# Moving the load of one batch's values behind the sort of the batch before it

## The chip, the cores and the metric

The kernel runs on one core of a Trainium2 chip. The metric is the device time of one execution in microseconds (us), median of the runs shown. The engines are named as in the profile: PE is TensorE, DVE VectorE, ACT ScalarE, POOL GpSimd, SP SyncE.

## The reference

Two stages follow each other: block-sorted attention, then a mixture of experts that every token passes through. Cut to what matters:

```python
# attention: B, H, S, D = 4, 8, 768, 64; 8 blocks of 96 tokens
P = sort_net
for _ in range(5):                       # Sinkhorn, over an 8x8 matrix per batch and head
    P = np.exp(P - P.max(-1, keepdims=True))
    P = P / (P.sum(-1, keepdims=True) + 1e-9)
    P = P / (P.sum(-2, keepdims=True) + 1e-9)
k_sorted = einsum('bhij,bhjcd->bhicd', P, k_blocks)
v_sorted = einsum('bhij,bhjcd->bhicd', P, v_blocks)
attn = softmax(q_blocks @ k_sorted^T / sqrt(D))      # inside each block
x = (attn @ v_sorted) -> (B*S, H*D) = (3072, 512)
# experts: E = 8, F = 1024
G = exp(logits - max), logits = x @ w_gate; 8 rounds of row and column scaling
out = sum_e G[:, e] * (relu(x @ w1[e]) @ w2[e])
```

All inputs and the output are float32 in HBM; the kernel works in bfloat16 with float32 accumulation.

## The kernel before

The attention stage goes batch by batch, numbered 0 to 3 in the code. Into its steps PE's work for expert 0 (`hidden0` L402, `output0` L411) on batches already attended is woven, so that PE has something to do while ACT and DVE empty its banks. Batch 0 has a prologue of its own. For batches 1 to 3 `attention` (L374) takes a plan of steps: `q` turns queries, `k` sorts keys, `s` makes scores, `m` mixes the sorted values, `t` or `T` turns the result (by PE, or by a transposing DMA from SP).

The steps around the change:

- `load_batch(bb, parts)` (L70) asks for queries, keys or values of a batch, 128 x 8 x 384 elements cast to bfloat16 on the way, by a DMA issued from POOL. Its tile `kvq` has five buffers, shared by all loads. The issue is pinned: it keeps its place in program order.
- `spread_r(bb)` (L151, by `build_r` L134) builds R, the matrices with which PE sorts keys and values of a batch: two multiplications on POOL of `Pb` (the finished P, spread over the partitions in the first stage) by a mask. They are pinned too. R has two buffers, one for even and one for odd batches.
- `sort_values(bb, bank)` (L162) sorts the values: eight matmuls on PE (L165, reading R and the loaded values), each emptied by ACT into `vs` (L167); then `hop(bb)` (L155) copies `vs` into `vsb`, eight small DMAs, four issued from SP and, for batches 2 and 3, four from POOL.
- `queries(bb, hp, bank)` (L174) reorders a pair of heads of batches 2 and 3 from the loaded queries into `qr` by a copy on POOL (L186) and turns them on PE (L190). The copies on POOL are not pinned: the scheduler puts them where it finds room between the pinned ones. `qr` has two buffers.

PE's order is pinned by hand throughout; POOL works off one queue in order, whose first member that waits holds up all behind it. At the place of the change the code runs the first steps of batch 1 (`run_both(at1, ...)`), asks for all of batch 2's loads (values, keys, queries), then for batch 3's values, spreads P for batch 2, goes on with batch 1's mixing steps, sorts the values of batch 2 and finishes batch 1 (L591 to L599). Keys and queries of batch 3 are asked for in the loop over batches 2 and 3, ahead of `spread_r(3)` (L608, L609).

Of the kernel before, what the change touches and what calls it, by code (L numbers as in the profile page):

```python
# [25 lines left out]
def kernel(  # L26
# [43 lines left out]
    def load_batch(bb, parts):  # L70
        for x, l0, n in parts:
            d, src = {"v": (vt, v), "k": (kt, k), "q": (qt, q)}[x]
            if bb not in d:
                d[bb] = kvp.tile([128, 8, 384], BF16, name="kvq", bufs=5)
            pin(nc.gpsimd.dma_start(
                out=d[bb][:, l0:l0 + n, :],
                in_=src[bb, l0:l0 + n].rearrange("h (p kk) d -> p h (kk d)", kk=6)))
# [4 lines left out]
    def load_w1(e, f0=0, f1=F):  # L82
        if e not in w1t:
            w1t[e] = wp.tile([128, 4, F], BF16, name="w1e")
        pin(nc.gpsimd.dma_start(
            out=w1t[e][:, :, f0:f1],
            in_=moe_w1[e].rearrange("(kk k) f -> k kk f", k=128)[:, :, f0:f1]))
# [63 lines left out]
    def spread_r(bb):  # L151
        for _ in build_r(bb, nc.gpsimd, 4):
            pass

    def hop(bb, pieces=None):  # L155
        for eng, i, h0, n in pieces or [(nc.gpsimd if i % 2 and bb > 1 else nc.sync, i, 0, 8)
                                        for i in range(NB)]:
            (pin if bb == 0 else lambda ins: ins)(eng.dma_start(
                out=mkap(vsbt[bb % 2], [[VW, 96], [1, 65 * n]], off=i * 520 + 65 * h0),
                in_=vs[16 * i:16 * i + 16, :, h0:h0 + n].rearrange("p kk h d -> p kk (h d)")))  # L160

    def sort_values(bb, bank):  # L162
        for h in range(8):
            vps = bank([128, 384], F32)
            pin(nc.tensor.matmul(vps, Rt[bb][:, h].rearrange("p i c -> p (i c)"),  # L165
                                 vt[bb][:, h, :], start=True, stop=True))
            nc.scalar.copy(vs[:, :, h, 0:64], vps.rearrange("p (kk d) -> p kk d", d=64))  # L167
            if h % 2:
                yield
        hop(bb)  # L170
# [203 lines left out]
    def attention(bb, bank, plan):  # L374

        def step(what, hp):
            if what == "q":
                queries(bb, hp, bank)
            elif what == "k":
                keys(bb, hp, bank)  # L380
            elif what == "s":
                scores(bb, hp, bank)
            elif what == "t":
                turn(bb, hp, bank, nc.vector.tensor_copy)
            elif what == "T":
                turn_by_dma(bb, hp)
            elif what == "x":
                next(x0)
            elif what == "L":
                logits(bb - 1, bank, range(4))  # L390
            elif what == "l":
                logits(bb, bank, (0, 1, 2) if hp == 0 else (3,))
            else:
                for h in range(2):
                    mix(bb, hp, h, bank)

        for some in plan.split():
            for x in some.split(","):
                step(x[0], int(x[1]))
            yield  # L400

    def hidden0(c0, hTs, hbank, fbs=range(8)):  # L402
        for fb in fbs:
            hps = hbank()
            for kk in range(4):
                pin(nc.tensor.matmul(hps[:, 0:384], w1t[0][:, kk, fb * 128:(fb + 1) * 128],  # L406
                                     xtT[:, kk, c0:c0 + 384], start=(kk == 0), stop=(kk == 3)))
            nc.scalar.activation(out=hTs[:, fb, 0:384], in_=hps[:, 0:384], func=AF.Relu)
            yield

    def output0(c0, hTs, obank, done, tts=range(3)):  # L411
        for tt in tts:
            oacc = obank()
            for fb in range(8):
                pin(nc.tensor.matmul(oacc, hTs[:, fb, tt * 128:(tt + 1) * 128],  # L415
                                     w2t[0][:, fb, :], start=(fb == 0), stop=(fb == 7)))
                if fb == 3:
                    yield
            done(c0 // 128 + tt, oacc)
            yield  # L420
# [10 lines left out]
    def sum_w(e):  # L431
        wct[e] = (wcq if e % 2 == 0 else wcp).tile([128, 3, 2, F // 2], BF16, name="wc")
        for kk in range(2):
            a11, a21 = (w1t[e][:, kk, f:f + 512] for f in (0, 512))
            a12, a22 = (w1t[e][:, 2 + kk, f:f + 512] for f in (0, 512))
            s1, s2, s4 = (wct[e][:, j, kk, :] for j in range(3))
            for a, b, o, c in ((a21, a22, ALU.add, s1), (s1, a11, ALU.subtract, s2),
                               (a11, a21, ALU.subtract, a21), (a12, s2, ALU.subtract, s4)):
                pin(nc.gpsimd.tensor_tensor(out=c, in0=a, in1=b, op=o))
                yield  # L440
# [105 lines left out]
    def weave(a, b, na, nb):  # L546

        t = 0
        for i in range(na):
            next(a, 0)  # L550
            while t * na < (i + 1) * nb:
                next(b, 0)
                t += 1

    with ExitStack() as c2:
        pa = c2.enter_context(tc.tile_pool(name="pa", bufs=8, space=bass.MemoryType.PSUM,
                                           reuse_waits="tile"))
        bank1 = lambda shape, dt: pa.tile(shape, dt, name="bank", tag="bank")
        ebank = lambda: bank1([128, 512], F32)
        def by_turns(x, y):  # L560
            for a, b in ((x, y), (x, y)):
                yield next(a)
                yield next(b)

        def first_two():
            yield from hidden0(384, halves[1], ebank, range(2, 8))
            for c0, hTs in ((0, halves[0]), (384, halves[1])):
                o = [output0(c0, hTs, ebank, keep, (tt,)) for tt in range(3)]
                if c0 == 0:
                    yield from by_turns(o[0], o[1])  # L570
                    yield from o[2]
                else:
                    for one in o:
                        yield from one
            for c0 in (S, S + 384):
                hTs = mps.tile([128, 8, 384], BF16, name="hTs")
                yield from hidden0(c0, hTs, ebank)
                yield from output0(c0, hTs, ebank, keep)

        ex = first_two()  # L580

        def run(n):
            for _ in range(n):
                next(ex)

        def run_both(a, counts):
            for n in counts:
                next(a, 0)
                run(n)

        at1 = attention(1, bank1, "k0 k1 q0 q1 s0 k2 q2 k3 q3 s1 s2 s3 "  # L591
                                  "m0 m1,t0 m2,t1 m3,t2 t3,l0 l3")
        run_both(at1, (1, 1, 1, 0, 1, 0, 0, 1, 0, 1, 0, 2))
        load_batch(2, [(x, 0, 8) for x in "vkq"])
        load_batch(3, [("v", 0, 8)])
        spread_r(2)
        run_both(at1, (2, 1, 1, 1))
        run_both(sort_values(2, bank1), (1, 0, 1, 0, 1))
        run_both(at1, (1, 1))  # L599
        for bb, plan, ns in (  # L600
                (2, "q0,q1,k0 k1,s0 q2,k2,s1 m0,T0 k3,s2,x0 q3,m1,T1,x0 s3,x0 m2,T2 m3,T3",
                 (6, 3, 2, 3)),
                (3, "q0,q1,k0 k1,s0 q2,k2,s1 m0,T0 k3,s2 q3,m1,T1 s3,L0 m2,T2 m3,T3",
                 (6, 4, 0, 4))):
            at1 = attention(bb, bank1, plan)
            weave(at1, ex, 5, ns[0])
            if bb + 1 < B:
                load_batch(bb + 1, [(x, 0, 8) for x in "kq"])  # L608
                spread_r(bb + 1)  # L609
            else:  # L610
                load_w1(1)
                sums = sum_w(1)
            weave(at1, ex, 3, ns[1])
            if bb + 1 < B:
                weave(sort_values(bb + 1, bank1), ex, 5, ns[2])
            else:
                for _ in sums:
                    pass
            weave(at1, ex, 1, ns[3])
        for _ in ex:  # L620
            pass
# [16 lines left out]
    def bank():  # L638
        return bk.tile([128, 512], F32, name="bk")
# [312 lines left out]
```

## Time and profile before

| | |
|---|---|
| median of 3 runs | 673.08 us (673.03 to 673.88) |
| the profiled execution, its time | 673.76 us |
| its span in the trace | 671.8 us |
| mean granted PE clock | 0.994 |
| busy: PE, DVE, POOL, ACT | 98%, 83%, 70%, 45% of the span |
| the attention stage | about the first 110 us |

In a timeline row stand the start in us from the span's start, the duration in us, engine, line, operation, the tiles written and read, the count (x), and in brackets the idle time of the engine ahead of it and what ended that. A row of waits has the engine and line that waited, what it waited for, the sum in us, how often and the longest. A row of a stretch (A:B) has its length, then busy time and count of PE, weight load, DVE, ACT and POOL, then granted PE clock, mean busy share of the DMA engines, and GB/s. A row of DMA issues has the count, KB of each, and the median us from issue to landing. In the clock row of the page each digit stands for a fortieth of the span, 9 for full speed.

### The profile page before, as it was taken

Reading aid. Unit: us, or ns where it says so; the run is one execution under the profiler, and the core shown is the slowest. Engines: PE = TensorE matmul, PEld = TensorE weight load, DVE = VectorE, ACT = ScalarE, POOL = GpSimd, SP = SyncE. Lnnn points to the kernel's source line nnn. Section 1 sums busy time; section 2 is a strip of 40 time slices with the busy share of each in tenths; the row PEclk is TensorE's granted clock in tenths of the full one; section 3 lists DMA queues with packets and bytes.
Section 4 is the critical chain, followed back from the end, with each engine's and each line's share of the span. In section 5 each row is a group of like instructions: output and inputs, shape, how many; then the busy total and the mean of one; then the engine's idle time right before and its main releaser. Section 6 shows DMA issues by size and latency. Waiting matters only on the chain.

```text
span 671.8 us, 13104 instructions
## 1 busy us (share of the span) xinstructions
PE 656.9 (98%) x5076; PEld 433.1 (64%) x5076; DVE 554.5 (83%) x1119; ACT 300.7 (45%) x535; POOL 470.5 (70%) x500
## 2 busy tenths in 40 slices
PE   7996999999999999999999999999999999999997
PEld 3763666554666666666666666666666666666666
DVE  6654566776888889898988989898989898989896
ACT  5772874477455434334333334333433343344330
POOL 4702435008997898898997898689886999646653
PEclk9997999999999999999999999999999999999999
DMA  9999996200340340031302140034003030001224
GB/s 187 175 220 133 144 138 88 48 1 2 62 64 1 63 63 1 1 64 9 55 1 35 30 63 2 1 63 63 1 0 64 6 59 1 1 1 52 76 95 157
DMA packets 39775, 38.53 MB, mean 57 GB/s; under 512 B 8512, under 2 KB 32800, under 8 KB 39712
## 3 DMA queue, kind: packets, MB, share of 16 engines
q0 software_dynamic: 26784, 27.03, 25.9%
q1 hardware_dynamic: 12816, 10.56, 6.4%
q8 instruction: 39, 0.64, 0.4%
q14 instruction: 24, 0.20, 0.1%
q10 hardware_dynamic: 112, 0.10, 0.1%
HBM read 52.45 MB, written 6.29 MB: 87 GB/s over the span
## 4 chain that ended last, share of the span: by engine, by line
PE 89%; ACT 0%; POOL 0%; DVE 0%; issue 0%; ACTq 0%
PE bk L701 38%; PE oacc L788 37%; PE oacc L415 3%; PE bk L406 3%; PE bank L415 2%; PE bank L406 2%; PE bank L244 1%; PE bk L788 1%; PE bank L226 1%; PE bank L165 1%; PE bank L204 1%; PE bk L824 1%; PE bank L190 0%; PE bank L275 0%; ACT atp L234 0%; POOL R L139 0%
## 5 line engine op out<-in xcount | busy, mean ns | idle before, releaser
L753 DVE SCALAR_TENSOR_TENSOR osbl<-oacc,glog,osbl 128x256 f32<-128x256 f32 (+1 forms) x490 | 255.9, 524 | 27.9 <-PE oacc L788 18.4
L701 PE MATMUL bk<-xtT,w1e 128*128 128x512 bf16 x504 | 148.6, 379 | 0.0
L771 POOL TENSOR_TENSOR hs<-hT 128x512 bf16<-128x512 bf16 (+2 forms) x105 | 98.4, 949 | 70.0 <-DVE hT L719 70.0
L788 PEld LDWEIGHTS <-hT 128*128 128x128 bf16 x996 | 97.4, 98 | 62.6 <-issue 0.2
L719 DVE CUSTOM_DVE_ANT_0 hT<-bk,p 128x512 bf16<-128x512 f32 x168 | 116.0, 691 | 26.1 <-PE bk L701 23.8
L788 PEld LDWEIGHTS <-hs 128*128 128x128 bf16 x996 | 97.4, 98 | 61.2 <-issue 1.6
L788 PE MATMUL oacc<-w2e,hT 128*128 128x256 bf16 x796 | 119.8, 273 | 0.0
L724 ACT COPY p<-bk 128x512 f32<-128x512 f32 x84 | 49.1, 585 | 147.5 <-PE bk L701 147.0
L771 POOL TENSOR_TENSOR hs<-hT,hs 128x512 bf16<-128x512 bf16 (+2 forms) x105 | 98.9, 950 | 4.7
L771 POOL TENSOR_TENSOR hs<-hs,hT 128x512 bf16<-128x512 bf16 (+2 forms) x105 | 99.0, 952 | 4.5 <-ACT hT L746 0.2
L701 PE MATMUL bk<-xc,wc 128*128 128x512 bf16 x336 | 99.8, 379 | 0.1
L746 ACT ACTIVATE hT<-bk 128x512 bf16<-128x512 f32 x84 | 50.1, 597 | 96.1 <-PE bk L701 96.1
L788 PE MATMUL oacc<-w2e,hs 128*128 128x256 bf16 x612 | 91.8, 273 | 0.0
L701 PEld LDWEIGHTS <-w1e 128*128 128x128 bf16 x672 | 65.7, 98 | 12.1
L719 DVE CUSTOM_DVE_ANT_0 hT<-bk,u 128x512 bf16<-128x512 f32 x84 | 58.0, 691 | 2.6 <-PE bk L701 2.6
L728 ACT COPY u<-bk 128x512 f32<-128x512 f32 x84 | 49.1, 585 | 23.9 <-PE bk L701 23.2
L733 ACT COPY p<-bk 128x512 f32<-128x512 f32 x84 | 49.2, 586 | 23.5 <-PE bk L701 23.5
L747 DVE SCALAR_TENSOR_TENSOR h<-bk,hT 128x512 bf16<-128x512 f32 x84 | 57.2, 681 | 2.6 <-ACT hT L746 2.6
L701 PEld LDWEIGHTS <-wc 128*128 128x128 bf16 x504 | 49.3, 98 | 8.1 <-issue 0.3
L788 PE MATMUL oacc<-w2s,hs 128*128 128x256 bf16 x364 | 53.3, 272 | 0.0
L701 PE MATMUL bk<-xc,w1e 128*128 128x512 bf16 x168 | 50.0, 379 | 0.0
L701 PE MATMUL bk<-xtT,wc 128*128 128x512 bf16 x168 | 50.0, 379 | 0.0
(148 smaller groups left out, 781.1 us busy)
## 6 DMA issues: line engine op xcount, KB each, us to landing
w1e<-in_moe_w_dram POOLq DMA_DIRECT2D x7, 1024.0 KB, 8.2
w2e<-in_moe_w_dram POOLq DMA_DIRECT2D x7, 1024.0 KB, 9.2
out_dram<-osbl SPq DMA_DIRECT2D x23, 256.0 KB, 2.1
kvq<-in_v_dram POOLq DMA_DIRECT2D x3, 768.0 KB, 10.1
kvq<-in_k_dram POOLq DMA_DIRECT2D x3, 768.0 KB, 11.0
vsb<-vs SPq DMA_DIRECT2D x18, 97.5 KB, 5.1
kvq<-in_q_dram POOLq DMA_DIRECT2D x4, 384.0 KB, 9.9
kvq<-in_q_dram POOLq DMA_DIRECT2D x2, 768.0 KB, 19.6
```

Of the source, the lines that this page charges most:

```text
L406: pin(nc.tensor.matmul(hps[:, 0:384], w1t[0][:, kk, fb * 128:(fb + 1) * 128], xtT[:, kk, c0:c0 + 384], start=(kk == 0), stop=(kk == 3)))
L415: pin(nc.tensor.matmul(oacc, hTs[:, fb, tt * 128:(tt + 1) * 128], w2t[0][:, fb, :], start=(fb == 0), stop=(fb == 7)))
L701: hold(nc.tensor.matmul(ps, wa[:, kk, :], xa[:, kk, :], start=(first and kk == 0), stop=(kk == 1), skip_group_check=True))
L719: nc.vector._custom_dve(TENSOR_ADD_SAT, out=out, in0=ps, in1=other, s0=TOP, s1=0.0)
L724: still(nc.scalar.copy(p1, u))
L728: still(nc.scalar.copy(u2, u))
L733: still(nc.scalar.copy(p5, v))
L746: still(nc.scalar.activation(out=c21, in_=u, func=AF.Relu))
L747: nc.vector.scalar_tensor_tensor(out=h3[e, p][:, i, :], in0=u, scalar=0.0, in1=c22, op0=ALU.max, op1=ALU.subtract)
L753: nc.vector.scalar_tensor_tensor(out=o, in0=ps, scalar=glog[:, t, e:e + 1], in1=o, op0=ALU.mult, op1=ALU.add)
L771: hold(nc.gpsimd.tensor_tensor(out=c, in0=a, in1=b, op=o))
L788: nc.tensor.matmul(ps, h[:, fb, :], w[:, fb, :], start=(first and fb == 0), stop=(fb == 3), skip_group_check=True)
```

## The change

The call that asks for batch 3's values moves from ahead of `spread_r(2)` to behind `sort_values(2, bank1)`, whose last step is the hop of batch 2. No instruction is added or taken away.

```diff
@@ -592,10 +592,10 @@
                                   "m0 m1,t0 m2,t1 m3,t2 t3,l0 l3")
         run_both(at1, (1, 1, 1, 0, 1, 0, 0, 1, 0, 1, 0, 2))
         load_batch(2, [(x, 0, 8) for x in "vkq"])
-        load_batch(3, [("v", 0, 8)])
         spread_r(2)
         run_both(at1, (2, 1, 1, 1))
         run_both(sort_values(2, bank1), (1, 0, 1, 0, 1))
+        load_batch(3, [("v", 0, 8)])
         run_both(at1, (1, 1))
         for bb, plan, ns in (
                 (2, "q0,q1,k0 k1,s0 q2,k2,s1 m0,T0 k3,s2,x0 q3,m1,T1,x0 s3,x0 m2,T2 m3,T3",
```

## The prediction

> Batches are numbered as in the code, from 0: "v3" is the load of the values of batch 3 (the fourth), R2 the spread of P for batch 2, a "hop" the copies of sorted values from vs to vsb.
>
> **What bounds the kernel now.** I read the page first, then TensorE's waits, then the queue of the engine it waits for.
>
> ```profile
> PE 656.9 (98%) x5076; PEld 433.1 (64%) x5076; DVE 554.5 (83%) x1119; ACT 300.7 (45%) x535; POOL 470.5 (70%) x500
> PEclk9997999999999999999999999999999999999999
> ```
>
> TensorE is busy 98% of the span, so nothing but a hole in its work, or a slow clock, can be won. The clock row has one digit under 9, the fourth slice (50.4 to 67.2 us). The waits of TensorE, longest first, name one hole:
>
> ```profile
> PE bank L165 <- POOL R L139: 6.2, 1, 6.2
> PE pair L298 <- DMA kvq<-in_q_dram: 1.2, 1, 1.2
> ```
>
> One wait of 6.2 us, and the next is five times smaller. L165 is the first matmul that sorts the values of batch 2, and it waits for R2, two multiplications on POOL. POOL's timeline shows why R2 is late:
>
> ```profile
> 34.13 0.88 POOL L75 DMA_DIRECT2D kvq<-in_q_dram  x1 [3.95 <-PE pair L285]
> 59.52 1.59 POOL L186 COPY qr<-kvq 128x768 bf16<-128x768 bf16 x2 [24.51 <-DMA kvq<-in_q_dram]
> 61.05 0.87 POOL L75 DMA_DIRECT2D kvq<-in_v_dram  x1
> 61.94 2.07 POOL L139 TENSOR_TENSOR R<-Pb,mask 128x512 bf16<-128x512 f32 x2
> 69.63 2.16 POOL L158 DMA_DIRECT2D vsb<-vs  x4 [5.61 <-issue]
> 72.19 0.82 POOL L186 COPY qr<-kvq 128x768 bf16<-128x768 bf16 x1 [0.40 <-PE bank L190]
> 72.95 0.92 POOL L75 DMA_DIRECT2D kvq<-in_k_dram  x1
> 73.87 0.90 POOL L75 DMA_DIRECT2D kvq<-in_q_dram  x1
> ...
> 87.91 1.60 POOL L186 COPY qr<-kvq 128x768 bf16<-128x768 bf16 x2 [10.29 <-DMA kvq<-in_q_dram]
> 90.09 2.21 POOL L158 DMA_DIRECT2D vsb<-vs  x4 [0.58 <-ACT vs L167]
> ```
>
> POOL works its queue in order. After the load of q2 (34.13) stand two copies of q2 into qr, which cannot start before q2 has landed; POOL idles 24.51 us for it, to 59.52. Only then come v3 and R2. R2 needs nothing of q2: it multiplies Pb, ready since the first batch, by a mask, and the buffer it writes was batch 0's. It is late because of its place in the queue.
>
> **The change, part by part.** The edit moves one call, load_batch(3, v), from before spread_r(2) to behind the sort and hop of batch 2. What counts is the order that the scheduler makes of it on POOL. Before: q2 load, two qr copies, v3, R2 (two), hop 2 (four). After: q2 load, R2 (two), two qr copies, hop 2 (four), v3, then as before a qr copy, k3, q3. So two things move: R2 goes ahead of the wait for q2, and v3 goes behind hop 2. The instructions of the other engines keep their order.
>
> *R2 early.* R2 now starts when the q2 load is issued, at 34.13 + 0.88 = 35.01, and ends near 37.1 by its own 2.07. The sort also needs v2 in place:
>
> ```profile
> 28.36 0.94 POOL L75 DMA_DIRECT2D kvq<-in_v_dram  x1
> kvq<-in_v_dram POOLq DMA_DIRECT2D x1, 768.0 KB, 23.3
> kvq<-in_q_dram POOLq DMA_DIRECT2D x1, 768.0 KB, 25.3
> 71.55 0.83 PE L190 MATMUL bank<-Ibig,qr 128*128 128x128 bf16 x12
> ```
>
> The first row is v2's issue, the second its landing, us from issue: near 51.7. The third is q2's, 34.13 + 25.3 = 59.4. TensorE reached the sort at 63.07 - 6.23 = 56.84 (first row of the chain below). v2 was in, R2 would have been ready for 19 us: the 6.23 us go, and what is late next, v2, is 5 us early. The qr copies stay at 59.52 and end at 61.11. Their reader, the turning of the queries (L190, the last row), moves by the 8.3 us worked out below from 71.55 to 63.2, so 2.1 us of cover remain.
>
> The same five steps (two, four and two sorting matmuls with four of L415 between) in batch 2 and in batch 3, from the chain of waits in order of time, give the second term:
>
> ```profile
> 63.07 0.82 PE bank L165 x2
> ...
> 67.85 0.33 PE bank L165 x2
> 68.18 0.86 PE bank L415 x4
> ...
> 85.92 0.33 PE bank L165 x2
> ...
> 88.94 0.71 PE bank L244 x16
> ```
>
> Batch 2 takes 68.18 - 63.07 = 5.11 us, batch 3 88.94 - 85.92 = 3.02 us. The difference, 2.09 us, is the clock:
>
> ```profile
> 60.00:61.00 1.00, 0.00 (x0) 0.00 (x0) 0.00 (x0) 0.00 (x0) 1.00 (x2) 0.58 0.00 0
> 62.00:63.00 1.00, 0.00 (x0) 0.00 (x0) 0.00 (x0) 0.00 (x0) 1.00 (x2) 0.50 0.43 16
> 66.00:67.00 1.00, 1.00 (x4) 0.45 (x3) 0.00 (x0) 1.00 (x4) 0.00 (x0) 0.51 1.32 205
> 67.00:68.00 1.00, 1.00 (x6) 0.49 (x5) 0.00 (x0) 0.76 (x2) 0.00 (x0) 1.00 0.61 91
> ```
>
> (The last three numbers of a row are granted clock, DMA share, GB/s.) The mean of 0.58 from 60 to 61 is one of full clock for 0.16 us and of half for the rest, so it fell at 60.16, 3.3 us into the hole, and was whole again 4 us after work resumed. Without the hole it has no reason to fall: gain 6.23 + 2.09 = 8.32 us. It could be less only if a new hole opens.
>
> The Trainium skill ("TensorE: Matmul & The Clock Gate", Part 1) has it that the clock halves after an idle window of about 3.4 us and returns after about 3.4 us of work; the trace agrees with 3.3 and 4. By that rule a remaining hole under 3.4 us costs its own length alone, a longer one 2.1 us besides, which is a rival below.
>
> *v3 late.* Two readers are in question: the sort of batch 3, and, since v3 now stands directly ahead of k3 and q3, the qr copies of batch 3.
>
> ```profile
> 85.75 0.49 PE L165 MATMUL bank<-kvq,R 128*128 128x384 bf16 x2
> 92.08 0.83 PE L190 MATMUL bank<-Ibig,qr 128*128 128x128 bf16 x12
> kvq<-in_v_dram POOLq DMA_DIRECT2D x1, 768.0 KB, 7.1
> kvq<-in_k_dram POOLq DMA_DIRECT2D x1, 768.0 KB, 10.8
> kvq<-in_q_dram POOLq DMA_DIRECT2D x1, 768.0 KB, 13.9
> 72.00:74.00 2.00, 2.00 (x27) 1.27 (x24) 1.06 (x2) 2.00 (x4) 1.81 (x3) 1.00 0.84 199
> 74.00:76.00 2.00, 2.00 (x38) 1.42 (x37) 1.06 (x2) 1.52 (x5) 1.99 (x3) 1.00 0.77 109
> ```
>
> (Two rows of TensorE's timeline; the landings of v3, k3 and q3 in us from issue; two stretches of DMA.) When is v3 issued? In batch 3 POOL's hop starts 90.09 - 85.75 = 4.34 us behind the first sorting matmul, so hop 2 starts near 56.84 + 4.34 = 61.2, just behind the qr copies, and v3 is issued at 61.2 + 2.2 = 63.4 (before: 61.05). Sorting of batch 3 moves from 85.75 to 77.4, so v3 may take 14.0 us. It took 7.1 on idle engines, and k3 took 10.8 behind a hop. Cost: nothing, with 3.2 us of cover by the dearer row.
>
> For q3 it is closer. k3 and q3 follow v3's issue (0.87) and a qr copy (0.82): k3 near 65.1, q3 near 66.0, which is 73.87 - 66.0 = 7.9 earlier than before while TensorE is 8.3 earlier: 0.4 of cover lost. The cover was 92.08 - (87.91 + 1.60) = 2.57 us, so 2.2 are left. Against it stand v3's bytes, which used to move while TensorE stood still and now share the engines with hop 2, k3 and q3. Lower bound of the delay: 0, if they fit where the engines have room. Upper bound: 4.0 us, the spacing at which k3 (72.95 + 10.8 = 83.75) and q3 (73.87 + 13.9 = 87.77) landed. Between: v3's packets come from about 64.7 on, 1.3 after issue (before, issued at 61.05, they began in the row of 62 to 63 us), that is 72.8 in the old time; from 72 to 76 the DMA share was 0.84 and 0.77 against 1.32 when full, room for 4 x (1.32 - 0.81) / 1.32 = 1.5 us. I take 4.0 - 1.5 = 2.5, an estimate from these rows. The wait is 2.5 - 2.2 = 0.3 us; its ends are 0 and 1.8.
>
> ```profile
> vsb<-vs POOLq DMA_DIRECT2D x2, 97.5 KB, 4.1
> 98.35 0.87 PE L244 MATMUL bank<-vsb,atp 96*96 96x65 bf16 x16
> ```
>
> Hop 3 on POOL stands behind q3's copies, so if q3 is 2.5 late, hop 3 is 2.5 + 0.4 - 0.6 = 2.3 late (it idled 0.58 for ACT). The fence has the landing of its last copies and their reader, the first mix of batch 3. The last of four issues begins near 91.8 and lands at 95.9, so 2.4 us of cover stand against 2.3; and what q3 adds beyond that TensorE has already waited at L190. No cost. SP's four copies of a hop go when vs is complete, as before.
>
> **Sum.** 8.32 - 0.3 = 8.0 us. The profiled execution has a span of 671.8 and a time of 673.76; the median of the three runs is 673.08, 0.7 lower. Against the median: 665.1. All that follows is released by TensorE's progress and shifts with it.
>
> **Rivals.**
> *Late queries* (chance 0.24): v3's bytes add their full 4.0 us to q3. The Trainium skill ("DMA: Bandwidth & Descriptors", Issuing engines are not separate DMA queues) speaks for it: DMAs issued by SP and POOL run on the same 16 engines and interleave, so moving a load does not make room. By the rows: 1.8 us of wait at L190, 666.6. I allow up to 3.0, just short of the clock's 3.3, since a transfer at work beside others can be slower than the spacing shows: 667.8.
> *Late queries that stop the clock* (0.05): the wait passes 3.3 us, so 2.1 us come on top: at 4 us 8.32 - 6.1 = 2.2 gained, 670.9. It needs q3 6.2 us later, more than a whole load.
> *No change* (0.03): the hole stays because R2 waits for something else that comes with q2's landing; the rows show no such thing. 673.1.
> *Slower: late values* (0.05): v3 lands later than 14.0 us after issue, and the sort of batch 3 waits as that of batch 2 does now. With the clock's 2.1 the gain is lost once the wait passes 6.2, a landing of 20.2 us. v2 took 23.3: then the wait is 9.3, the cost 11.4, the time 676.2. Against it: v2 stood behind a backlog of whole loads, v3 only behind a hop; in the queue k3 and q3 are behind it.
>
> **How the numbers follow.** The forecast has 0.63, and its time is the prediction. The range goes from 664.0 (8.3 won, no wait, and 0.8 for the spread between runs, 673.03 to 673.88) to 668.0 (late queries at their worst): it leaves out about 0.15. A measurement here tells about 0.2% (1.3 us) from no change: faster 0.63 + 0.24 + 0.05 = 0.92, same 0.03, slower 0.05.
>
> **What would show it.** In the changed profile: POOL's R at about 35 us ahead of its long wait for q2; no wait of PE at L165 for R; the fourth digit of the clock row at 9; 0.33 us for two sorting matmuls of batch 2 in the chain; v3 issued near 63.4 and landed before 77; q3 landing near 82, and a wait at L190 of batch 3 of under 2 us. A clock digit under 9 in the fourth or fifth slice, or a wait at L165 for the load of v, would make it wrong.

## The result

The changed kernel takes 667.01 us (median of 21 runs, 665.13 to 673.47) against 673.88 us for the kernel before (21 runs, 672.51 to 694.25). The ratio is 0.9901, with a 95% interval of 0.988 to 0.9921: 6.7 us gained, 5.3 to 8.1 by the interval. Forecast were 8.0 us and 665.1. An execution more than 1.5% above the fastest of its kernel is left out of every ratio and, in the experiments, of every difference between medians. The profiled execution of the changed kernel has a span of 663.4 us, 8.4 less than the 671.8 before, and is the fastest of its kind.

The same rows of the page, and the longest waits of PE, in the changed kernel:

```profile
PE 654.2 (99%) x5076; PEld 432.5 (65%) x5076; DVE 553.8 (83%) x1119; ACT 300.3 (45%) x535; POOL 470.6 (71%) x500
PEclk9999999999999999999999999999999999999999
```

```profile
PE pair L298 <- DMA kvq<-in_q_dram: 1.9, 1, 1.9
PE pair L337 <- DVE blank L104: 1.2, 1, 1.2
```

The wait at L165 is gone, and the clock row has no digit under 9. The longest waits that are left lie in the first 20 us, ahead of the change. POOL's timeline shows the new order:

```profile
33.99 0.88 POOL L75 DMA_DIRECT2D kvq<-in_q_dram  x1 [3.97 <-PE pair L285]
34.88 2.08 POOL L139 TENSOR_TENSOR R<-Pb,mask 128x512 bf16<-128x512 f32 x2
59.02 1.59 POOL L186 COPY qr<-kvq 128x768 bf16<-128x768 bf16 x2 [22.05 <-DMA kvq<-in_q_dram]
61.47 2.16 POOL L158 DMA_DIRECT2D vsb<-vs  x4 [0.87 <-POOL qr L186]
63.64 0.93 POOL L75 DMA_DIRECT2D kvq<-in_v_dram  x1
64.56 0.83 POOL L186 COPY qr<-kvq 128x768 bf16<-128x768 bf16 x1
65.33 0.89 POOL L75 DMA_DIRECT2D kvq<-in_k_dram  x1
66.21 0.89 POOL L75 DMA_DIRECT2D kvq<-in_q_dram  x1
...
81.48 1.60 POOL L186 COPY qr<-kvq 128x768 bf16<-128x768 bf16 x2 [11.53 <-DMA kvq<-in_q_dram]
83.02 2.13 POOL L158 DMA_DIRECT2D vsb<-vs  x4
```

R2 stands ahead of the long wait, at 34.88 instead of 61.94; v3 is issued at 63.64 instead of 61.05. PE's timeline carries both terms of the sum:

```profile
55.67 1.03 PE L415 MATMUL bank<-w2e,hTs 128*128 128x512 bf16 x4
56.54 0.49 PE L165 MATMUL bank<-kvq,R 128*128 128x384 bf16 x2
...
59.56 1.03 PE L415 MATMUL bank<-w2e,hTs 128*128 128x512 bf16 x4
...
63.10 0.83 PE L190 MATMUL bank<-Ibig,qr 128*128 128x128 bf16 x12
...
83.63 0.83 PE L190 MATMUL bank<-Ibig,qr 128*128 128x128 bf16 x12
```

The sort follows the work ahead of it without a gap, and its five steps take 59.56 - 56.54 = 3.02 us where they took 5.11. L190 of batch 2 moved from 71.55 to 63.10, 8.45 us; L190 of batch 3 from 92.08 to 83.63, again 8.45. Nothing was given back between them in this execution. The two copies ahead of the second L190 ended at 83.08, though: 0.55 us of cover.

That one execution gains 8.4 us and the medians 6.9 is the open point. The spans of the changed kernel spread: over the 33 executions of the three times it was run, 663.4 to 675.4 us with a median of 665.5. Where these 2 us come from is what most of the experiments ask.

### The profile page after: what moved, and what is told of

Read it like the earlier page. It is cut to its first block, busy times and chain, and to the rows that moved or that the text cites. A ratio compares the mean times of both kernels' runs of the same rounds, so it can differ in the third digit from the quotient of the medians.

```text
span 663.4 us, 13104 instructions
## 1 busy us (share of the span) xinstructions
PE 654.2 (99%) x5076; PEld 432.5 (65%) x5076; DVE 553.8 (83%) x1119; ACT 300.3 (45%) x535; POOL 470.6 (71%) x500
## 4 chain that ended last, share of the span: by engine, by line
PE 95%; DVE 1%; ACT 1%; DMA 1%; issue 0%; ACTq 0%; SPq 0%; DVEq 0%
PE bk L701 38%; PE oacc L788 38%; PE bank L415 3%; PE oacc L415 3%; PE bk L406 3%; PE bank L406 2%; PE bank L244 1%; PE pair L370 1%; PE bank L204 1%; PE bank L226 1%; DMA osbl<-in_k_dram 1%; PE bk L788 1%; PE bk L824 1%; PE bank L165 0%; PE pair L346 0%
## 5 line engine op out<-in xcount | busy, mean ns | idle before, releaser
L788 PEld LDWEIGHTS <-hs 128*128 128x128 bf16 x996 | 97.4, 98 | 61.2 <-issue 1.6
## 6 DMA issues: line engine op xcount, KB each, us to landing
kvq<-in_k_dram POOLq DMA_DIRECT2D x3, 768.0 KB, 10.7
```

What stands on the lines that cost most here:

```text
L788: nc.tensor.matmul(ps, h[:, fb, :], w[:, fb, :], start=(first and fb == 0), stop=(fb == 3), skip_group_check=True)
```

## The experiments

Each edit is made to the kernel named. Times are medians, and ratios stand against the kernel before, run beside it on the same chip. Where the text compares a kernel with the changed kernel, it compares medians of executions that were measured together.

### The changed kernel again, twice

No edit.

> The changed kernel once more, for the spread of its times beside the others of this call. Theory A: R2 early is the whole gain, and some executions lose part of it because q3 lands later than the 0.55 us of cover that the first profile left (copies done 83.08, reader at 83.63); then its profiles show either no wait of PE over 1.9 us (time near 665) or a wait at L190 of batch 3. Rival B: the spread has nothing to do with the moved load, and kernels without it behind the hop spread as much. Median 666 to 668.

667.42 us (668.0 with one execution of 677.37; ratio 0.9909, 0.9874 to 0.9944). In this profiled execution (span 665.5) q3 landed 16.9 us after issue instead of 15.1, and PE waited for its copies; from PE's timeline:

```profile
85.00 0.51 PE L190 MATMUL bank<-Ibig,qr 128*128 128x128 bf16 x6 [0.33 <-POOL qr L186]
85.77 0.51 PE L190 MATMUL bank<-Ibig,qr 128*128 128x128 bf16 x6 [0.26 <-POOL qr L186]
```

0.6 us in all: the wait that the prediction feared, at its place. It is only a part of the 2.1 us by which this span is longer than the first. The sort of batch 2 began at 57.41 instead of 56.54, so 0.9 us had been lost ahead of the changed stretch, 0.7 of them at L285, where PE waited for the values of batch 1.

> The changed kernel a third time, as measure for the three beside it and for its spread. Theory A (late queries make the spread): most executions between 665.5 and 669, a median of 667 to 668; the profile shows a wait of PE at L190 of 0 to 2 us. Rival B: as the kernel with v3 ahead of the copies.

667.71 us (ratio 0.9884, 0.9842 to 0.9927). The profile this time caught a late execution, with a span of 672.3. Its waits of PE:

```profile
PE bank L275 <- DMA xtT<-og: 4.3, 1, 4.3
PE pair L337 <- DVE blank L104: 1.2, 1, 1.2
PE bank L244 <- DMA vsb<-vs: 1.1, 1, 1.1
```

The issue of the transposing DMA in SP's timeline:

```profile
85.66 2.60 SPq L261 DMA_TRANSPOSE xtT<-og  x1
```

The landings of that DMA and of the load beside it, us from issue:

```profile
w1e<-in_moe_w_dram POOLq DMA_DIRECT2D x1, 1024.0 KB, 15.8
xtT<-og SPq DMA_TRANSPOSE x1, 16.6
```

And two stretches:

```profile
92.00:94.00 2.00, 2.00 (x37) 1.33 (x35) 1.91 (x8) 1.80 (x6) 0.00 (x0) 1.00 1.23 27
102.00:104.00 2.00, 1.65 (x10) 0.79 (x11) 0.21 (x1) 0.00 (x0) 1.60 (x2) 0.54 0.89 119
```

None of it is a wait for queries. The last transposing DMA of batch 2 (L261), issued at 85.66, landed after 16.6 us, where it took 5.8 in the first profile; the 1 MB load of expert 1's first weights beside it took 15.8 us instead of 10.7. From 92 to 94 us the DMA engines are busy (share 1.23) and move 27 GB/s. L275, the routing logits of batch 2, waits 4.3 us for that transposed block, and the clock falls behind it (0.54). The hop of batch 2 was late too: 1.1 us at L244, the first mix. So three transfers of this stretch can be late, not one, and my theory A for the spread was too narrow.

### R2 first, v3 ahead of hop 2

```diff
 (before)
-        load_batch(3, [("v", 0, 8)])
         spread_r(2)
+        load_batch(3, [("v", 0, 8)])
```

> R2 ahead of everything, v3 asked for ahead of hop 2 instead of behind it (about 61 instead of 63.6). Theory A: the same 8.4 us by the profile, since the order of R2 is what counts: span near 663.4, no wait at L165. v3 lands near 68 instead of 72, q3 not later than 81.3. Rival: if the place of v3 behind the hop was part of the gain, this one is slower by over 1 us.

668.88 us (669.62 with one execution of 678.28; ratio 0.9939, 0.9906 to 0.9973), 1.5 over the changed kernel beside it. In the profile (span 664.6) v3 is issued at 60.66, R2 is early, L165 does not wait. Most of the gain is there without moving v3 behind the hop, so R2's place is its cause. But the hop, four of whose copies now stand behind v3 in POOL's queue, is late for the mix:

```profile
70.24 0.55 PE L244 MATMUL bank<-vsb,atp 96*96 96x65 bf16 x3 [0.17 <-DMA vsb<-vs]
71.00 0.60 PE L244 MATMUL bank<-vsb,atp 96*96 96x65 bf16 x10 [0.20 <-DMA vsb<-vs]
```

In this profile SP's four copies of the hop landed 7.2 us after issue (median) and POOL's four 7.9, against 3.9 and 3.5 in the first profile of the changed kernel. PE took 1.0 us longer from the second L190 of batch 2 to the third (67.51 to 73.78, against 67.33 to 72.62). So the rival has a part in it in this execution: v3's place behind the hop is worth about 1 us once R2 is early. By the medians that isn't shown, since the intervals of the two ratios overlap. The hop's cover is thin in any case: it was 1.1 us short in the late execution above even with v3 behind it.

### R2 late, v3 still behind hop 2

```diff
 (changed kernel)
         load_batch(2, [(x, 0, 8) for x in "vkq"])
+        pin(nc.gpsimd.tensor_copy(held, qt[2][0:96, 0, 0:2]))
         spread_r(2)
```

> v3 stays behind hop 2, but R2 is held behind the landing of q2 by a tiny copy out of q2 (96x2) ahead of it. Theory A: the wait at L165 comes back, R's first half ends near 60.3, a hole of 3.8 us instead of 6.2; the clock falls only after 3.3 us of it and costs 0 to 2.1. Slower than the changed kernel by 3.8 to 5.9 us, 668 to 671. Rival: if v3's place made the gain, as fast as the changed kernel.

673.73 us (673.74 with one execution of 682.17; ratio 0.9986, 0.9961 to 1.0011): the whole gain is gone with this one small copy, although v3 is where the change puts it. The sort waits again, and the clock falls. PE's wait, and the first and the last row of the sort in the chain:

```profile
PE bank L165 <- POOL R L139: 3.9, 1, 3.9
...
60.69 0.50 PE bank L165 x2
...
65.57 0.86 PE bank L415 x4
```

Three stretches:

```profile
61.00:62.00 1.00, 1.00 (x5) 0.40 (x3) 0.00 (x0) 0.87 (x2) 1.00 (x2) 0.61 0.00 0
62.00:63.00 1.00, 1.00 (x4) 0.45 (x3) 0.00 (x0) 0.23 (x1) 1.00 (x2) 0.50 0.00 0
64.00:65.00 1.00, 1.00 (x5) 0.35 (x3) 0.00 (x0) 0.90 (x3) 0.00 (x0) 0.69 0.00 0
```

The hole is 3.87 us (3.8 expected), and the five steps, from 60.69 to 65.57 in the chain, take 4.88 us, 1.86 more than at full clock. With 0.7 us at L190 of batch 3 that makes 6.4 of the 6.8 us by which this span (670.2) exceeds the changed kernel's first. The hole and the clock explain that much, and no more: this execution is the fastest of its twelve, and where the median loses another 1.8 us, which makes it equal to the kernel before, no trace shows.

### A short hole

```diff
 (changed kernel)
         load_batch(2, [(x, 0, 8) for x in "vkq"])
+        for _ in range(4):
+            pin(nc.gpsimd.tensor_copy(blank, kt[2][:, 0:2]... [:, 0:512]))
         spread_r(2)
```

> The changed kernel with R2 held back less far: four copies on POOL out of batch 2's keys (128x512 each) stand ahead of R2, so that R2 follows the landing of k2 (near 55.4) and not of q2. R's first half ends near 58.9, a hole of some 2.3 us at L165 (1.7 to 2.8 by the unknown length of the copies). Theory A: a hole that ends before the clock falls costs its own length and no more: the sort's five steps take 3.0 us, not 4.9 or 5.1, and the time is that of the changed kernel plus 2 to 3 us, less what the wait at L190 of batch 3 gets back. Rival: any hole at this place brings the half clock: plus 4 to 5 us.

670.88 us (ratio 0.9952, 0.9927 to 0.9977); span of the profiled execution 666.7, mean clock 1.0. From PE's timeline:

```profile
59.10 0.50 PE L165 MATMUL bank<-kvq,R 128*128 128x384 bf16 x2 [2.31 <-POOL R L139]
...
62.14 1.03 PE L415 MATMUL bank<-w2e,hTs 128*128 128x512 bf16 x4
```

A hole of 2.31 us, and the five steps take 62.14 - 59.10 = 3.04: no clock was lost in this execution. Span against the changed kernel's first: 3.3 us, of which 2.3 are the hole, 0.3 a wait at L190 and 0.3 one at L244. So the 8.4 us are two things, the length of the hole and a half clock that can follow it and costs some 2 us. That a short hole is always spared the clock is not shown: this execution is the fastest of its ten, and seven of the ten have a mean clock under 0.999 (ten of the changed kernel's 33). No trace shows where it fell in them.

### More load in front of q3

```diff
 (changed kernel; a second one likewise, from v[3, 4:8])
         load_batch(3, [("v", 0, 8)])
+        pin(nc.gpsimd.dma_start(out=osbl[0]...[:, 6144:7680]..., in_=v[3, 0:4]...))
```

> One more load directly behind v3: 4 heads of values as float32 into a part of osbl that is written later (768 KB written, as v3; half as much read), otherwise the changed kernel. Theory A: q3 lands 3.5 to 4 us later, near 85, and PE waits 2.3 to 3.3 us at L190 of batch 3, under the 3.3 at which the clock falls: slower than the changed kernel by 2.3 to 3.5 us. Rival: the engines have room, or the cover is larger than 0.55: no wait, the same time.

671.11 us (671.44 with executions of 677.72 and 1376.1; ratio 0.9947, 0.9912 to 0.9982), 3.4 over the changed kernel beside it. q3 landed 19.5 us after issue, at 86.7, and PE waited 4.0 us at L190 of batch 3. (Nothing here explains the execution of 1376 us.)

> Two such loads behind v3. Theory A: q3 lands 7 to 8 us later, PE waits 6.5 to 7.5 us at L190 of batch 3, and now the clock falls too, 2.1 us more: slower than the changed kernel by 8 to 10 us, 674 to 677, that is as slow as the kernel before or slower. Rival without the clock: slower by 6.5 to 7.5.

679.5 us (ratio 1.0052, 1.0017 to 1.0087), 11.8 over the changed kernel and slower than the kernel before. Waits of PE and the clock row with one load more:

```profile
PE bank L190 <- POOL qr L186: 4.0, 2, 3.7
PEclk9999989999999999999999999999999999999999
```

and with two, with a stretch behind the wait at L275 besides:

```profile
PE bank L190 <- POOL qr L186: 4.7, 1, 4.7
PE bk L275 <- DMA xtT<-og: 3.0, 1, 3.0
...
PE bank L244 <- DMA vsb<-vs: 0.7, 1, 0.7
...
PEclk9999979999999999999999999999999999999999
...
118.00:120.00 2.00, 2.00 (x15) 1.34 (x14) 0.41 (x2) 1.34 (x3) 0.00 (x0) 1.00 0.75 123
```

One more load of v3's size takes the cover at L190 and more, as theory A has it, but dearer than I expected. The clock fell behind the wait (the 8 in the row), so the span is 5.8 us longer than the changed kernel's first: 4.0 of wait and some 1.8 of clock, by the time from the first L190 of batch 3 to its next turn of queries (87.73 to 93.98, against 83.63 to 87.87, less the second wait of 0.26). With two loads, q3 was less late than expected (4.7 us of wait, not 6.5 to 7.5). Some 2.7 us went to the clock behind it (89.37 to 96.36), 0.7 to the hop, and 3.0 to L275 at 117.33. This L275 reads the transposed blocks of batch 3, 40 us after the added loads had landed; that the loads made it late is not shown. The clock stayed whole behind this wait (1.00 in the stretch).

### v3 taken away, and v3 moved into the idle time

```diff
 (changed kernel; the sort of batch 3 reads batch 2's values)
-        load_batch(3, [("v", 0, 8)])
+        vt[3] = vt[2]
```

> The changed kernel without the load of v3 (the sort of batch 3 takes batch 2's values again; this leaves out a load and changes the output). Theory A: v3's bytes are what makes q3 late behind hop 2; without them q3 lands near 78 and nothing waits at L190 of batch 3: median 665.3 to 666, as the kernel with v3 ahead of the copies, and as narrow. Rival: q3 is late for k3's or the transposing DMAs' sake: median 667 to 668 as the changed kernel.

668.0 us (ratio 0.9915, 0.9884 to 0.9945). The landing of q3, us from issue, first here and then in the first profile of the changed kernel:

```profile
kvq<-in_q_dram POOLq DMA_DIRECT2D x1, 768.0 KB, 12.2
kvq<-in_q_dram POOLq DMA_DIRECT2D x1, 768.0 KB, 15.1
```

q3 landed at 65.53 + 12.2 = 77.7, where it landed at 66.21 + 15.1 = 81.3 with v3: 3.6 us, 0.7 of them from its later issue, and no wait is left at L190. But the time did not become narrower: the profiled execution (span 666.6) waits 1.5 us at L275 for the transposed block, which landed 13.9 us after issue. From PE's timeline, and a stretch:

```profile
98.32 0.30 PE L275 MATMUL bank<-wg,xtT 128*128 128x8 bf16 x6 [1.54 <-DMA xtT<-og]
100.00:102.00 2.00, 2.00 (x13) 0.95 (x11) 1.60 (x7) 0.00 (x0) 1.92 (x3) 0.51 0.18 39
```

This short wait was not spared the clock. It fell near 100.0, 1.7 us after PE had gone back to work, and from L275 to L664 (96.18 to 111.48, against 96.08 to 108.09 in the changed kernel's first profile) PE lost 3.3 us, 1.5 of wait and some 1.8 of clock. Theory A holds for q3 and fails for the whole of the spread.

```diff
 (before; reorder() makes qr and the copy that queries() made)
-        load_batch(3, [("v", 0, 8)])
         spread_r(2)
+        load_batch(3, [("v", 0, 8)]); ahead2.update({(2, hp): reorder(2, hp, pin) for hp in (0, 1)})
...
-            qr = sp.tile([128, 6, 2, 64], BF16, name="qr", bufs=2)
-            nc.gpsimd.tensor_copy(...)
+            qr = ahead2[bb, hp] if (bb, hp) in ahead2 else reorder(bb, hp)
```

> R2 first, then v3, and only then the two copies of q2 (pinned): v3 is issued near 43, when its buffer comes free, and travels behind q2 at 59 to 63, in the time in which the DMA engines stood idle. Theory A: q3 lands 3 to 4 us earlier (77 to 78), the cover at L190 of batch 3 grows from 0.55 to about 4 us; profile as the changed kernel (span 663 to 664), and, if late queries make the spread, a narrower spread and a median 1 to 2 us lower. Rival B: same median and same spread as the changed kernel.

665.56 us (ratio 0.988, 0.9845 to 0.9915) against 667.42 for the changed kernel beside it. POOL's timeline:

```profile
35.11 2.08 POOL L139 TENSOR_TENSOR R<-Pb,mask 128x512 bf16<-128x512 f32 x2
43.00 0.94 POOL L75 DMA_DIRECT2D kvq<-in_v_dram  x1 [5.81 <-PE bank L211]
59.73 1.58 POOL L176 COPY qr<-kvq 128x768 bf16<-128x768 bf16 x2 [15.79 <-DMA kvq<-in_q_dram]
61.70 2.15 POOL L158 DMA_DIRECT2D vsb<-vs  x4 [0.39 <-POOL qr L176]
...
78.15 1.60 POOL L176 COPY qr<-kvq 128x768 bf16<-128x768 bf16 x2 [8.76 <-PE bank L165]
```

v3 goes out as soon as its buffer is free and travels behind q2. The copies of q3 end at 79.75, 4.1 us ahead of their reader (83.86) instead of 0.55.

> v3 ahead of the copies of q2 once more, on the same chip as the changed kernel. Theory A: median 1 to 2.5 us under the changed kernel, most executions within 0.5 us of 665.5, no wait at the turning of batch 3's queries. Rival B (the spread comes from elsewhere): the same median and spread as the changed kernel.

665.92 us (ratio 0.9882, 0.9836 to 0.9928) against 667.71. Of the eleven spans of this kernel, eight lie between 663.4 and 663.7, the others at 664.5, 666.7 and 671.4; of the changed kernel's 33, three do.

### Expert 1's weights out of the way of the transposed block

```diff
 (changed kernel, and the kernel with v3 ahead of the copies)
-                load_w1(1)
-                sums = sum_w(1)
...
-                for _ in sums:
-                    pass
+                pin(nc.gpsimd.tensor_copy(held, xtT[0:96, 3, 2 * S:2 * S + 2])); load_w1(1)
+                for _ in sum_w(1): pass
```

> The changed kernel with the load of expert 1's first weights (1 MB, from POOL) held behind the landing of the last transposing DMA of batch 2 by a tiny copy out of xtT. Theory A (late queries make the spread): nothing changes, spans between 663.5 and 668 as before, a median span near 665.5. Theory C (in some executions that transposing DMA, asked for 0.8 to 1.5 us ahead of the 1 MB load and running beside it, lands 14 to 17 us after issue, and PE waits for it at L275): the waits at L275 go, spans over 668 become rare; a spread of up to 2 us from the queries stays. Median span 664.5 to 665.5.

667.03 us (666.75 to 669.8; ratio 0.9907, 0.988 to 0.9934). Spans 665.0 to 668.0. What stays is the wait for the queries, 1.4 us in the profiled execution (span 665.1):

```profile
PE bank L190 <- POOL qr L186: 1.4, 2, 1.1
```

> Both: v3 ahead of the copies of q2, and expert 1's first weights behind the landing of batch 2's last transposing DMA. Theory C with A: both sources are gone, all spans within 663.4 to 664.5, median time near 665.4. If spans of 666 and more still come as often as in the two runs with v3 ahead alone (2 in 11), the slow stretch of the DMA engines is not the 1 MB load's doing.

665.33 us (665.26 to 665.55; ratio 0.9869, 0.9848 to 0.989): the lowest median, 1.7 us under the kernel above beside it, and all six spans between 663.5 and 663.6. With both edits no execution was late. That the 1 MB load was the cause of the late block is not shown by this: spans over 668 were 5 in 33 of the changed kernel, 3 in 10 without v3 and 1 in 11 with v3 ahead, so none in 12 with the load held back can be chance. What makes the DMA engines busy at 27 GB/s in such a stretch stays open.

## Why the prediction was right, and where it was off

The time lies in the range, and the main mechanism came out to within 0.3 us: R2 at 34.88 (35.0 forecast), no wait at L165, five steps in 3.02 us, L190 of batch 2 at 63.10 (63.2), v3 issued at 63.64 (63.4). The term of 8.32 us was 8.45 in the first profile, which is the fastest of 33 executions, so some of this closeness is luck. Holding R2 back brought the hole and the old time back with v3 left in its new place; making R2 early without moving v3 behind the hop kept most of the gain. The median came out 1.9 us over the forecast. 0.8 of that is the starting point, 673.08 then and 673.88 now; the gain fell short by 1.1.

The clock's share is shown as a term of its own at L165: 2.31 us of hole without it, 3.87 us with 1.86 of it, 6.23 us with 2.09. The limit that the prediction made of it does not hold. It let a hole under 3.4 us cost its own length alone, and without v3 a hole of 1.54 us at L275 cost 3.3. The clock fell 3.3 us into the hole of the kernel before, but 4.4 us after the beginning of the shorter one (61.2 against 56.8), when PE had been at work again for half a us; a hole of 3.00 us, with two loads more, brought no half clock at all. The Trainium skill ("TensorE: Matmul & The Clock Gate", Part 1) says that the window is free-running. The traces agree in this, that a fall does not keep a fixed distance from the hole's beginning; but the idle window of about 3.4 us that the prediction took from the same part was not needed at the hole of 1.54. The term of 2.09 us was read from the trace of the hole itself and does not rest on this limit.

*Late queries.* The forecast has q3 take 2.5 us longer than the 13.9 before, against 2.2 us of cover: 0.3 us of wait. In the four profiles with R2 early and one load of values directly ahead (the changed kernel three times, and once with expert 1's weights held back) it took 14.9 to 17.7 us, 1.0 to 3.8 longer, and PE waited 0, 0.6, 0 and 1.4 us. The first profile had 1.8 us of cover, of which 1.2 were used. So the size of the term was fair; what it missed is that one number stood for a delay that differs by 2.8 us between executions. What v3's bytes cost is known to a us or two only: without a load of values beside it (no v3, and v3 ahead of the copies, in four profiles) q3 took 12.2 to 14.4 us. The rival of this name, 666.6 us, is nearer to the median of 667.0 than my forecast is, and I gave it 0.24. The Trainium skill's rule behind it ("DMA: Bandwidth & Descriptors", Issuing engines are not separate DMA queues) is that loads from all queues interleave on the same engines. The trace agrees where v3, issued from POOL, stands ahead of the hop: SP's four copies then took 7.2 us instead of 3.9 to 4.4.

*Not in the sum at all* were two more readers of this stretch. I looked for who waits for v3 and for who stands behind it in POOL's queue, and did not ask which transfers of other queues share the engines with it. The hop of batch 2 was given no cover by number and can be 1.1 us late for L244; the last transposing DMA of batch 2, issued from SP, can be 4.3 us late for L275, clock besides. The second is not v3's alone, since it came without v3 too, and its cause stays open. Nor is all of the spread in this stretch: the second profile had lost 0.9 us ahead of it.

*Late values*, the rival that would have made it slower, did not come: v3 landed 8.4 us after issue in the first profile, 14.0 allowed. Slower than before it became with two loads added, and by way of the queries, the clock, the hop and the transposed blocks of batch 3, not of the values.

## What to carry to other kernels

On an engine that works its queue in order, look first at what a late instruction stands behind: here two multiplications that needed nothing new stood behind copies that waited 24.5 us for a load, and a move of an unrelated load let them pass. When a hole closes, every transfer that ran beside it loses that cover, so list all readers of the same stretch, of every queue, with their cover in us, and move loads into the time in which the DMA engines stand idle. Price a hole at its length and, as long as no trace says otherwise, at a half clock of some 2 us besides: here one of 1.54 us brought it and one of 3.00 did not. If one execution gains more than the medians, profile the kernel again until a late one is caught.

## What was not expected of the hardware

- In some executions the DMA engines were busy and moved almost nothing for some 6 us (share 1.23 at 27 GB/s, from 92 to 94 us, where the first profile has 1.08 at 181 GB/s); a transposing DMA of 5.8 us then took 13.9 or 16.6.
- The clock can fall after work has resumed: at 61.2 us, with matmuls running since 60.69, behind a hole of 3.87 us; and near 100.0 us, with matmuls running since 98.32, behind one of 1.54.
- SP's four copies of the hop landed 7.2 us after issue with a load from POOL ahead of them, and 3.9 to 4.4 in the three profiles of the changed kernel, where that load comes later.
